# Scores of four more units from the split form in a recurrence with a feed-forward layer, on one core

## The chip, the cores and the metric

The kernel runs on one core of one Trainium2 chip. The metric is the device time of one execution in microseconds. Before the change it is 342.12 us, the median of three runs (340.52 to 343.04).

## The reference, cut to what matters

The first half is a gated linear recurrence, worked through in chunks of 32 tokens: 4 batches of 8 heads with 768 tokens, head width 32 and state width 16. The second half is a feed-forward layer with softplus on the 3072 rows that the first half gives.

```python
CB = np.einsum('bhin,bhjn->bhij', Cc, Bc)          # the scores
M = CB * L                                         # weighed with the decays, causal
y_intra = np.einsum('bhij,bhjd->bhid', M, xc)
y_inter = np.einsum('bhin,bhnd->bhid', Cc, state) * decay_to_i[:, :, :, None]
...
h = x @ w_in                                       # 256 -> 2048
g = np.maximum(h, 0.0) + np.log1p(np.exp(-np.abs(h)))
return (g @ w_out).astype(np.float32)              # 2048 -> 256
```

## The kernel before, in words

**Units.** The recurrence is cut into 24 units of 128 tokens of one batch, all 8 heads at once (unit i is batch i // 6, place i % 6). A unit's inputs are one load into a tile un: its tokens' x and B by token, C by row, and what the scores are made of. A unit goes through: rm, the causal decays, on POOL (`decays`, L345); the scores sp, two blocks of 128x512 for four heads each (`score`, L378); m, their product with rm, on DVE (`weigh`, L402); bp and cc, B and C scaled, on DVE (`scale_b`, L360, and `scale_c`, L376); zp and the new state (`update`, L416 and L428); tb, the state spread over two heads (`spread`, L436); the output yp, from the state (`read`, L450) and from m (`within`, L466); y, with the growth factors gg (L477), and its high and low parts xh and xl (L480, L485), which the layer reads.

**Two forms of scores.** Units 0 to 11 (`i < FIRST`) take each block as one plain float32 product: 64 rows of B against 512 columns of C that the host has laid out apart for each head (L386; units 0 to 3 from a tile of their own). Their load comes from the array fst, 576 KB a unit. Units 12 to 23 take the split form. Their load comes from the array un, 768 KB, with B and C stacked so that each number stands in several rows. `split_unit` makes from them, with one pass on ACT (L247) and one on DVE (L248) each, the tiles c_all and b_rows, which hold a number's high part in some rows and its low part in others. Two DMAs copy c_all into c_rows (L254, by the helper at L136), where each copy fills the rows of one of two heads and the rest stays zero. Then four products of 128 rows against 256 columns (L391) give the same two blocks. There is only one c_rows: it can be filled for a unit when the scores of the unit before have been taken. c_all and b_rows have two buffers each, un has three.

**The layer.** Six token blocks j of 512 tokens and 16 slices k of the 2048 hidden columns. For each (j, k) there are six products into hp (`first`, L563), with the weights' and the tokens' high and low parts wih, wil, xh, xl; then e, softplus, on ACT (L591), its high part gh on ACT (L597) and its low part gl on DVE (L603); then six products into the two sums acc (`second`, `block`, L642). The weights w_in and w_out arrive as 64-bit numbers; for each of 16 steps ACT and DVE turn them into high and low parts (`split_stages`): even steps make wih and wil, step 12 those of slices 12 and 13; odd steps make woh and wol. Tiles for e have three buffers, for gh and gl four.

**Order.** All loads, copies and stores go through one queue, issued by SP in the order of the list. Up to unit 7, and to the weights' last step, the order is written by hand (the table ORDER; its instructions appear at L127, the helper that records them, whatever function made them). From unit 8 on, and from the layer's step 20, the order is a plan: a loop over steps s (one (j, k) each) plans for unit 8 the scores at step 20, for units 9, 10 and 11 at 22, 25 and 28, for later ones every fourth step; the output part comes one step later for units 8 to 11 and two for the others; the load of unit i + 2 comes one step after unit i's scores (L767 to L773). Within that plan a scheduler places the instructions on each engine, so that an edit can move other work; instructions of the hand-written part and of the plan stand mixed on the engines around 76 to 92 us.

Of the kernel before, what the change touches and what calls it, by code (L numbers as in the profile page):

```python
# [26 lines left out]
NFT = DFF // P  # L27
TOK = NB * S
HEAD = 4
FIRST = 12  # L30
GU = 3
U_X = 0
U_B = U_X + DM
# [71 lines left out]
def recurrence_then_ffn(ctx: ExitStack, tc: tile.TileContext, fst, un, at, al, w_in, w_out, const, outT):  # L105
# [28 lines left out]
    def load(out, in_):  # L134

        tc.keep_in_program_order(nc.sync.dma_start(out, in_))  # L136
# [73 lines left out]
    def load_unit(i):  # L210
# [4 lines left out]
        un_s[i] = p3.tile([P, U_END], F32, tag="un", name=f"un{i}")  # L215
        if i < FIRST:
            load(un_s[i][:, :F_END], fst[i])
        else:
            load(un_s[i], un[i - FIRST])

# [17 lines left out]
    def split_unit(i):  # L238
        if i < FIRST:
            return  # L240
        t = un_s[i]
        b_rows = p2.tile([P, NQ, P], F32R, tag="b_rows", name=f"b_rows{i}")

        def split(out, j):
            raw = t[:, U_S + j * NQ * P : U_S + (j + 1) * NQ * P].rearrange("p (q t) -> p q t", q=NQ)
            g, be = (kb[:, C_GB + v : C_GB + v + 1] for v in (2 * j, 2 * j + 1))
            A.activation(out, raw, AF.Copy, scale=be)  # L247
            V.scalar_tensor_tensor(out, raw, g, out.bitcast(F32), op0=ALU.mult, op1=ALU.add)  # L248

        c_all = p2.tile([P, NQ, P], F32R, tag="c_all", name=f"c_all{i}")  # L250
        split(c_all, 1)
        for e in range(2):
            rows = slice(64 * e, 64 * e + 64)
            load(c_rows[rows, :, e].bitcast(F32), c_all[rows].bitcast(F32))  # L254
        split(b_rows, 0)
        st[i] = b_rows
# [121 lines left out]
    def score(i, g):  # L378
        sp = mid[i]["sp", g] = ps.tile([P, 512], F32, tag="ps", name=f"sp{i}_{g}")
        if i < FIRST:  # L380
            rows = slice(64 * g, 64 * g + 64)
# [452 lines left out]
```

## Time and profile before

| | |
|---|---|
| median of three runs | 342.12 us (340.52 to 343.04) |
| the profiled execution | 340.56 us, its span 338.8 us |
| PE busy | 328.7 us, 97% of the span |
| DVE, ACT, POOL busy | 202.8 (60%), 171.7 (51%), 39.3 (12%) us |
| chain that ended last | PE 86%, DVE 6%, DMA 5% |
| loads from fst, from un | 8 of 576 KB, 12 of 768 KB |
| granted TensorE clock | 1.00 |

How to read the rows: PE is the matrix engine's products, PEld its weight loads, DVE the vector engine, ACT the scalar engine, POOL GpSimd, SPq the queue of SyncE, which issues the DMAs. A row of a timeline has the start in us, the length in us, the engine, the line, the operation, what it writes <- what it reads, shapes, how many were merged, and in brackets how long the engine sat idle before it and what ended that. In these rows tiles have no numbers. A float32 product shows as two instructions. A product's length contains the pipeline's fill, so that lengths overlap; prices are taken from start to start. A window's row has its bounds and length, then the busy time and count of PE, PEld, DVE, ACT and POOL, the granted clock, the share of the 16 DMA engines' time and GB/s. A row of waits has who waited, for whom, the sum in us, how often, and the longest. A row of DMA issues has the number, the KB of each and the median us from issue to landing.

### The profile page before, as it was taken

The page shows a single profiled execution, that of the slowest core. Times are in us where ns is not written, and L with a number is a line of the kernel's source. Part 1 is how long each engine was busy: PE and PEld are TensorE (multiplying, and loading weights), DVE is VectorE, ACT ScalarE, POOL GpSimd, SP SyncE. Part 2 cuts the span into 40 slices and gives each one's busy share as a digit, 9 for nine tenths or more (in the row PEclk, how much of TensorE's full clock was granted, in tenths as well). Part 3 has the DMA queues.
Part 4 walks back from the last instruction along what each step waited for, and adds up shares of the span by engine and source line. Part 5 has one row for each costly group of instructions (what it writes and reads, how often), then busy time and mean ns, then how long its engine had stood idle before and what let it go on. Part 6 is the DMA issues. An engine that isn't in the chain of part 4 may idle for free.

```text
span 338.8 us, 5271 instructions
## 1 busy us (share of the span) xinstructions
PE 328.7 (97%) x2047; PEld 249.4 (74%) x2047; DVE 202.8 (60%) x394; ACT 171.7 (51%) x319; POOL 39.3 (12%) x32
## 2 busy tenths in 40 slices
PE   8789998999999999999999999999999999999995
PEld 4446657887666678778778778778778778888885
DVE  0899989996946444864765464777474342232242
ACT  4845666875715435445445455445445244444450
POOL 2434510000111010110112010111010000000000
PEclk9999999999999999999999999999999999999999
DMA  7964533573032205416434205443203100010001
GB/s 233 396 228 138 220 106 104 188 259 120 3 98 114 93 0 189 133 39 186 126 61 141 95 0 188 122 106 99 94 2 93 33 0 0 2 55 8 2 0 62
DMA packets 19376, 35.01 MB, mean 103 GB/s; under 512 B 1432, under 2 KB 10136, under 8 KB 19352
## 3 DMA queue, kind: packets, MB, share of 16 engines
q1 hardware_dynamic: 19352, 34.68, 31.5%
q8 instruction: 16, 0.26, 0.3%
q14 instruction: 8, 0.07, 0.1%
HBM read 28.28 MB, written 3.24 MB: 93 GB/s over the span
## 4 chain that ended last, share of the span: by engine, by line
PE 86%; DVE 6%; DMA 5%; SPq 1%; issue 1%; ACT 0%
PE hp L563 32%; PE acc L642 32%; PE hp L127 6%; PE acc L127 6%; PE yp L466 3%; DMA gg<-gd 3%; DMA head_in_l<-in_fst 2%; PE yp L450 2%; PE sp L391 2%; DVE m L127 1%; DVE w L127 1%; PE sp L386 1%; SPq L136 1%; PE zp L416 1%; PE end L127 1%
## 5 line engine op out<-in xcount | busy, mean ns | idle before, releaser
L603 DVE TENSOR_TENSOR gl<-e,gh 128x512 fp32r<-128x512 f32 x76 | 55.7, 734 | 61.3 <-ACT gh L597 61.1
L597 ACT CAST gh<-e 128x512 fp32r<-128x512 f32 x76 | 47.1, 620 | 61.1 <-PE acc L642 60.3
L591 ACT ACTIVATE e<-hp 128x512 f32<-128x512 f32 x76 | 45.1, 596 | 42.4 <-DVE gl L603 38.5
L563 PE MATMUL hp<-xh,wih 128*128 128x512 f32 x152 | 61.3, 405 | 0.0
L642 PE MATMUL acc<-gl,woh 128*128 128x512 f32 x155 | 60.6, 391 | 0.0
L642 PE MATMUL acc<-gh,wol 128*128 128x512 f32 x155 | 60.5, 391 | 0.0
L642 PE MATMUL acc<-gh,woh 128*128 128x512 f32 x155 | 59.6, 391 | 0.0
L563 PE MATMUL hp<-xl,wih 128*128 128x512 f32 x152 | 59.5, 392 | 0.0
L563 PE MATMUL hp<-xh,wil 128*128 128x512 f32 x152 | 59.3, 391 | 0.0
L345 POOL TENSOR_SCALAR_AFFINE_SELECT rm<-fc 128x1024 f32<-128x1024 f32 x16 | 23.8, 1487 | 187.7 <-DVE m L402 167.8
L563 PEld LDWEIGHTS hp<-xh,wih 128*128 128x128 f32 x152 | 28.5, 188 | 10.7 <-issue 3.1
L642 PEld LDWEIGHTS acc<-gh,woh 128*128 128x128 f32 x155 | 29.1, 188 | 6.8 <-issue 0.8
L642 PEld LDWEIGHTS acc<-gh,wol 128*128 128x128 f32 x155 | 29.1, 188 | 6.2
L642 PEld LDWEIGHTS acc<-gl,woh 128*128 128x128 f32 x155 | 29.1, 188 | 6.1 <-issue 0.2
L563 PEld LDWEIGHTS hp<-xh,wil 128*128 128x128 f32 x152 | 28.5, 188 | 6.3
L563 PEld LDWEIGHTS hp<-xl,wih 128*128 128x128 f32 x152 | 28.6, 188 | 5.1
L402 DVE TENSOR_TENSOR m<-sp,rm 128x512 f32<-128x512 f32 x32 | 20.9, 685 | 7.9 <-PE sp L391 6.3
L127 DVE SCALAR_TENSOR_TENSOR w<-wraw,w 128x512 int32<-128x512 int32 x32 | 23.1, 729 | 0.2
L127 PE MATMUL hp<-xh,wih 128*128 128x512 f32 (+1 forms) x48 | 17.7, 368 | 2.0 <-DVE m L127 1.4
L127 PE MATMUL hp<-xl,wih 128*128 128x512 f32 (+1 forms) x48 | 17.0, 354 | 0.0
L127 PE MATMUL hp<-xh,wil 128*128 128x512 f32 (+1 forms) x48 | 17.0, 354 | 0.0
L127 POOL TENSOR_SCALAR_AFFINE_SELECT rm<-fc 128x1024 f32<-128x1024 f32 x8 | 14.0, 1764 | 20.8 <-DVE m L127 15.0
(109 smaller groups left out, 409.6 us busy)
## 6 DMA issues: line engine op xcount, KB each, us to landing
un<-in_un SPq DMA_DIRECT2D x12, 768.0 KB, 4.4
un<-in_fst SPq DMA_DIRECT2D x8, 576.0 KB, 6.1
wraw<-in_w_in SPq DMA_DIRECT2D x8, 512.0 KB, 3.4
wraw<-in_w_out SPq DMA_DIRECT2D x8, 512.0 KB, 5.2
c_rows<-c_all SPq DMA_DIRECT2D x24, 128.0 KB, 2.4
out_t<-o SPq DMA_DIRECT2D x11, 256.0 KB
gg<-gd SPq DMA_DIRECT2D x14, 192.0 KB
head_in_l<-in_fst SPq DMA_DIRECT2D x4, 320.0 KB, 6.2
```

Source lines behind the costliest of these rows:

```text
L127: return lambda *a, **k: tc.keep_in_program_order(f(*a, **k))
L136: tc.keep_in_program_order(nc.sync.dma_start(out, in_))
L345: Pl.affine_select(out=rm.rearrange("p h c i -> p (h c) i"), in_=fc[:, u].rearrange("p h c -> p (h c)").unsqueeze(2).broadcast_to([P, NH * ...
L391: PE.matmul(sp[:, 2 * v * P : 2 * (v + 1) * P], b_rows[:, q], c_rows[:, q].rearrange("p e t -> p (e t)"), start=True, stop=True,)
L402: V.tensor_tensor(mid[i]["m"][:, 4 * g : 4 * g + 4].rearrange("p h t -> p (h t)"), mid[i].pop(("sp", g)), mid[i]["rm"][:, 4 * g : 4 * g + ...
L450: PE.matmul(yp[q // 2][out], tb[rows].rearrange("p e d -> p (e d)"), cc[rows].rearrange("p c i -> p (c i)"), start=True, stop=False,)
L466: PE.matmul(yp[g][32 * hh : 32 * hh + 32], un_s[i][:, U_X + h * D : U_X + (h + 1) * D], m[:, h, :], start=u == 0, stop=True,)
L563: PE.matmul(h[:, c0:c1], w[:, c, fs], x[:, c, c0:c1], start=i == 0, stop=i == 5)
L591: A.activation(e, h, AF.Softplus)
L597: A.copy(gh, e)
L603: V.tensor_tensor(gl, e, gh.bitcast(F32), op=ALU.subtract)
L642: PE.matmul(acc[:, c0:c1], wo[v, k // HK][:, k % HK, es], g[:, c0:c1], start=start and i == 0, stop=stop and i == 2,)
```

## The change

The number of the first unit in split form goes from 12 to 8.

```diff
-FIRST = 12
+FIRST = 8
```

All that depends on it follows: the host puts units 8 to 11 into the array un instead of fst; `load_unit` loads 768 KB for each of them instead of 576; `split_unit`, which returned at once for them, now makes c_all and b_rows and copies into c_rows; `score` takes the four products from c_rows and b_rows instead of two from un.

```python
def split_unit(i):
    if i < FIRST:
        return
...
def score(i, g):
    sp = mid[i]["sp", g] = ps.tile([P, 512], F32, tag="ps", name=f"sp{i}_{g}")
    if i < FIRST:
...
```

How this moves instructions is shown at three places. In the rows, un10 is unit 10's tile, gh1_7 the gh of j = 1, k = 7; the last number is the tile's own and means nothing.

SP, after the last weights. Before:

```order
L136 DMA un8_1062<-in_fst 128x1152
L136 DMA un9_1064<-in_fst 128x1152
L136 DMA gg9_1066<-gd_84 128x1x384 x2
L136 DMA un10_1138<-in_fst 128x1152
L136 DMA un11_1207<-in_fst 128x1152
L136 DMA un12_1309<-in_un 128x1536
```

And now:

```order
L136 DMA un8_1062<-in_un 128x1536
L136 DMA un9_1064<-in_un 128x1536
L136 DMA gg9_1066<-gd_84 128x1x384 x2
L136 DMA c_rows_86<-c_all8_1083 64x4x128 x2
L136 DMA un10_1148<-in_un 128x1536
L136 DMA c_rows_86<-c_all9_1164 64x4x128 x2
L136 DMA un11_1227<-in_un 128x1536
L136 DMA c_rows_86<-c_all10_1270 64x4x128 x2
L136 DMA un12_1339<-in_un 128x1536
```

Two copies into c_rows stand ahead of each load from un10 on.

ACT, where the hand-written part ends. Here e, gh and half belong to the layer, woh1 and wih to the weights (w15 and w12 are their steps 15 and 12). Before:

```order
L127 CAST gh1_6_988<-e1_6_892 128x512
L127 ACTIVATE e0_9_997<-hp0_9_910 128x512
L127 CAST woh1_855<-w15_952 128x512
L127 CAST gh1_7_1003<-e1_7_984 128x512
L127 ACTIVATE e0_11_1014<-hp0_11_934 128x512
L127 CAST wih_78<-w12_956 128x2x256
```

And now:

```order
L127 CAST gh1_6_988<-e1_6_892 128x512
L247 ACTIVATE c_all10_1270<-un10_1148,kb_77 128x512
L127 ACTIVATE e0_9_997<-hp0_9_910 128x512
L127 CAST woh1_855<-w15_952 128x512
L127 CAST gh1_7_1003<-e1_7_984 128x512
L127 ACTIVATE e0_11_1014<-hp0_11_934 128x512
L127 CAST wih_78<-w12_956 128x2x256
```

The pass for c_all10, which reads un10, stands ahead of five others. (On DVE, gl1_6 has gone from behind bp10 and cc10, which read un10, to ahead of them.)

PE, unit 8's state and output. Before, with zp8 on its own eight products into hp earlier:

```order
L416 MATMUL zp8_1110<-un8_1062,bp8_1091 32x64 x4
...
L450 MATMUL yp8_0_1117<-cc8_1093,tb8_1108 64x128 x2
L450 MATMUL yp8_1_1118<-cc8_1093,tb8_1108 64x128 x2
L466 MATMUL yp8_0_1117<-m8_1086,un8_1062 32x128 x4
L466 MATMUL yp8_1_1118<-m8_1086,un8_1062 32x128 x4
```

And now:

```order
L416 MATMUL zp8_1120<-un8_1062,bp8_1101 32x64 x4
L450 MATMUL yp8_0_1127<-cc8_1103,tb8_1118 64x128 x2
L466 MATMUL yp8_0_1127<-m8_1095,un8_1062 32x128 x4
L450 MATMUL yp8_1_1128<-cc8_1103,tb8_1118 64x128 x2
L466 MATMUL yp8_1_1128<-m8_1095,un8_1062 32x128 x4
```

The parts from the state (L450) and from m (L466) now alternate, directly behind zp8. Before, it was unit 10's that alternated; now unit 9's are cut by one product into hp.

## The prediction

> **What bounds the kernel now.** I read first the page's busy times and the chain that ended last, then busy time by stage, then the timelines of PE, ACT, DVE and the DMA issues around the first four planned units.
>
> ```profile
> PE 328.7 (97%) x2047; PEld 249.4 (74%) x2047; DVE 202.8 (60%) x394; ACT 171.7 (51%) x319; POOL 39.3 (12%) x32
> PE 86%; DVE 6%; DMA 5%; SPq 1%; issue 1%; ACT 0%
> ```
>
> ```profile
> 77.00:86.00 9.00, 9.00 (x47) 7.05 (x46) 6.65 (x15) 5.47 (x11) 0.00 (x0) 1.00 0.35 103
> 86.00:123.00 37.00, 37.00 (x247) 24.07 (x246) 22.46 (x47) 17.57 (x32) 5.13 (x4) 1.00 0.20 70
> 134.00:275.00 141.00, 141.00 (x905) 111.12 (x904) 85.39 (x162) 68.28 (x121) 15.44 (x10) 1.00 0.31 91
> ```
>
> In the windows the third number is PE's busy time: it equals the window's length in all three. Units 8 to 11 are scored in the second. So from 77 us on PE has no idle time to absorb anything: a microsecond taken from PE's work there comes off the end, and a microsecond that PE is made to wait is added to it. DVE (22.46 of 37) and ACT (17.57 of 37) have room as sums, but each works through its own list in order, so what counts is where a late input stands in the list.
>
> **What the change removes from PE.** The price of a score block is the start-to-start time across it, less that of two ordinary 128x512 products.
>
> ```profile
> 94.28 0.40 PE L563 MATMUL hp<-xh,wil 128*128 128x512 f32 x1
> 94.60 1.13 PE L386 MATMUL sp<-un 64*128 64x512 f32 x4
> 95.66 0.50 PE L642 MATMUL acc<-gh,woh 128*128 128x512 f32 x1
> 96.00 0.40 PE L642 MATMUL acc<-gl,woh 128*128 128x512 f32 x1
> ```
>
> ```profile
> 133.61 0.39 PE L642 MATMUL acc<-gh,wol 128*128 128x512 f32 x1
> 133.84 0.64 PE L391 MATMUL sp<-c_rows,b_rows 128*128 128x256 f32 x4
> 134.31 0.40 PE L563 MATMUL hp<-xh,wih 128*128 128x512 f32 x1
> 134.54 0.40 PE L563 MATMUL hp<-xl,wih 128*128 128x512 f32 x1
> ```
>
> Ordinary products start 0.227 us apart (133.61 to 133.84 is such a step). Plain scores of unit 9: 96.00 - 94.28 - 2 x 0.227 = 1.27 us. Split scores of unit 12: 134.54 - 133.61 - 2 x 0.227 = 0.48 us. Four units save 4 x 0.79 = **3.2 us** of PE.
>
> [...]
>
> **What the reorder costs PE.** The scheduler also places the output products anew. Unit 8's, in one piece before, are now interleaved (state part, own part, state part, own part); unit 10's, interleaved before, no longer are.
>
> ```profile
> 98.39 0.45 PE L450 MATMUL yp<-cc,tb 32*64 32x128 f32 x8
> 99.34 0.50 PE L563 MATMUL hp<-xh,wih 128*128 128x512 f32 x1
> ```
>
> ```profile
> 109.53 0.43 PE L450 MATMUL yp<-cc,tb 32*64 32x128 f32 x4
> 110.23 0.43 PE L450 MATMUL yp<-cc,tb 32*64 32x128 f32 x4
> 111.16 0.50 PE L563 MATMUL hp<-xh,wih 128*128 128x512 f32 x1
> ```
>
> In one piece 99.34 - 98.39 = 0.95 us, interleaved 111.16 - 109.53 = 1.63 us. Units 8 and 10 exchange that 0.68, and unit 9's block is newly cut by one hidden-layer product. Bounds: 0 (they cancel) to +0.7 (one more interleaved block). I take **+0.4**: the exchange cancels, and unit 9's single cut is priced at a little over half of the 0.68 that two cuts cost.
>
> **What it adds, and what hides it.** Per unit two passes on ACT, two on DVE, two copies into c_rows, and 192 KB more in the load.
>
> ```profile
> 103.73 0.72 ACT L247 ACTIVATE c_all<-un,kb 128x512 fp32r<-128x512 f32 x1 [0.19 <-DMA un<-in_un]
> 104.36 0.71 ACT L247 ACTIVATE b_rows<-un,kb 128x512 fp32r<-128x512 f32 x1
> 104.49 0.75 DVE L248 SCALAR_TENSOR_TENSOR c_all<-un,kb,c_all 128x512 fp32r<-128x512 f32 x1 [0.46 <-ACT c_all L247]
> ```
>
> As work this is 4 x 1.43 = 5.7 us of ACT and some 6 us of DVE, beside 19 us and 14 us idle on them in 86 to 123: nothing, with that cover. If the cover were gone (every pass in PE's way) it would be 12 us; I see no place for that, except one.
>
> **The new wait.** ACT's list now has c_all10 ahead of e0_9, woh1 (step 15), gh1_7, e0_11 and wih (step 12). c_all10 cannot start before un10 has landed, and the five behind it wait with it. Two of them are PE's: acc takes gh1_7, and hp0_12, the product right after, takes wih of step 12.
>
> ```profile
> 79.50 0.62 ACT L127 CAST gh<-e 128x512 fp32r<-128x512 f32 x1 [1.22 <-PE acc L127]
> 80.03 0.59 ACT L127 ACTIVATE e<-hp 128x512 f32<-128x512 f32 x1
> 81.39 0.59 ACT L127 ACTIVATE e<-hp 128x512 f32<-128x512 f32 x1
> 81.88 0.61 ACT L127 CAST woh<-w 128x512 fp32r<-128x512 f32 x1
> 82.39 0.62 ACT L127 CAST gh<-e 128x512 fp32r<-128x512 f32 x1
> 84.83 0.60 ACT L127 ACTIVATE e<-hp 128x512 f32<-128x512 f32 x1 [1.82 <-DVE gl L127]
> 85.44 0.62 ACT L127 CAST wih<-w 128x512 fp32r<-128x512 f32 x1
> ```
>
> ```profile
> 83.71 0.29 DVE L360 TENSOR_TENSOR bp<-un,ft 128x128 f32<-128x128 f32 x1 [2.26 <-DMA un<-in_fst]
> ```
>
> ```profile
> 86.35 0.39 PE L563 MATMUL hp<-xh,wih 128*128 128x512 f32 x1
> ```
>
> ```profile
> ACT c_all L247 <- DMA un<-in_un: 11.9, 11, 2.4
> ```
>
> Before, un10 (landed by 83.71) held up bp10 on DVE, gl1_6 behind it, and so e0_11; wih ended at 85.44 + 0.62 = 86.06 and PE took it at 86.35: a margin of 0.29 us. That such a pass idles ACT until its load is in, the last row shows for the later units (11 waits). Now, from un10's landing to the end of wih: c_all10 0.63 (103.73 to 104.36), e0_9 0.49 (81.39 to 81.88), woh1 0.51, gh1_7 0.53 (79.50 to 80.03), e0_11 0.61, wih 0.62, together **3.4 us**. The copies and the DVE passes for e0_11 and wih are ready earlier: gl1_6 now stands ahead of bp10, and the last DVE pass for step 12, behind bp10 and another short one, ends about 1.2 us after the landing (an estimate: 0.2 us for each short one, about 0.7 for the pass).
>
> **When un10 lands.** It waits for unit 7's buffer as before, but stands on SP behind the two copies into c_rows.
>
> ```profile
> 77.94 0.33 SPq L136 DMA_DIRECT2D un<-in_fst  x1
> ```
>
> ```profile
> 72.00:77.00 5.00, 5.00 (x23) 4.13 (x22) 4.51 (x9) 3.71 (x7) 0.00 (x0) 1.00 0.89 345
> ```
>
> ```profile
> 135.80:137.30 1.50, 1.50 (x9) 1.23 (x8) 1.50 (x3) 1.50 (x4) 0.30 (x1) 1.00 0.86 172
> 104.00:108.00 4.00, 4.00 (x17) 2.63 (x17) 3.24 (x6) 2.18 (x4) 0.14 (x1) 1.00 0.22 76
> ```
>
> ```profile
> un<-in_un SPq DMA_DIRECT2D x12, 768.0 KB, 4.4
> un<-in_fst SPq DMA_DIRECT2D x8, 576.0 KB, 6.1
> c_rows<-c_all SPq DMA_DIRECT2D x24, 128.0 KB, 2.4
> ```
>
> Issued at 77.94, un10 took 5.8 us, because the growth factors (two gg copies) were still in the queue: the last window, after un12 has landed, shows such a pair keep 0.22 of the DMA engines busy for 4 us at 76 GB/s. My reading is that un10's share on those few engines comes after gg. Then what is put ahead adds up there: un8 and un9 192 KB more each at 345 GB/s, 1.1 us; the c_rows pair 1.5 us (the 135.80 window, 172 GB/s, holds nearly that pair alone); un10's own 192 KB, 0.6 us. Landing at 83.7 + 1.1 + 1.5 + 0.6 = 86.9. Bounds: 83.7 (all of it passes on engines that are free) and 90.2 (the two copies cost their landing time of 2.4 us each instead of 1.5 together). I take 86.9, because every term has a row of the same kind of transfer.
>
> hp0_12 then starts at 86.9 + 3.4 = 90.3 instead of 86.35: **+4.0 us** (0.8 to 7.3 by the bounds). What is late next: sp8 needs c_rows8, which is ahead of un10 in the queue and so in by then. gl1_7, the step-12 wil and m8 come off DVE some 3 to 6 us after the landing, counting its list at 0.6 to 0.75 us a pass, and PE, counting its list at 0.227 us a product, asks for them 5 to 8 us after it. From there c_rows9 waits for sp8, un11 behind it for unit 8's products, and m9's second half, on DVE behind c_all11, for un11: with the 4.4 us of the un row and one pass each on ACT and DVE it is done about 1 us before PE asks for it. These are estimates from the rows shown, and I take nothing for them.
>
> **Sum.** 340.56 (profiled execution, span 338.8 and 1.76 around it) + 4.0 - 3.2 + 0.4 = 341.8, +1.2 us. Against the median of the runs, 342.12, that is **343.3 us**. A measurement tells about 1% (3.4 us) from no change, so this is no change.
>
> **The rivals.**
>
> *The load is not late (340.1 us).* un10 lands at 83.7 as before. For it: at a share of 0.22, some 12 of the 16 DMA engines are free in the gg tail. Against: un10's own 5.8 us in that tail. Price: 83.7 + 3.4 - 86.35 = 0.8 us of wait, net -2.0; with no wait at all -2.8, or 339.3.
> [...]
>
> *The copies block the queue (346.6 us, slower).* One mechanism: the c_rows pair, in small pieces, goes at 2.4 us a copy on the engines that gg holds, and un10 lands at 90.2. hp0_12 waits 7.3 us, net +4.5. It decides (over 1%) once un10 lands after 89.1. For it: the landing time of 2.4 us. Against: the pair took 1.5 us together at 135.80, with no gg beside it.
>
> *The wait ends elsewhere, no net change (342.1 us).* The saved 3.2 us come back as small waits at m9, m10 and yp, whose inputs now hang on c_rows and on loads behind it in SP's list. For it: the slack of about 1 us at m9. Against: no single one is long.
>
> **How the numbers follow.** Forecast 0.55, load not late 0.25, copies block 0.12, scattered waits 0.08. Faster by over 1% needs more than the whole PE saving without any wait: only the far edge of the second case, 0.06. Slower by over 1%: the third case and the edge of the forecast, 0.14. Same 0.80. The range goes from the second case's 340.1, a little below for the spread of the runs (339.8), to 345.5, short of the third case.
>
> **What would show it.** Right: sp of units 8 to 11 as L391 rows with 0.48 us each; c_all10 on ACT idle before it for 3 us or more, released by the load of un10; then one PE gap of 3 to 5 us just ahead of acc with gh1_7 and hp0_12, between 85 and 92 us, and none as long after it; PE full again from there, the end shifted by the gap less 2.8. Wrong: no PE gap there (second case); a gap over 6 us (third); a bp10 that starts before 85 us; or gaps at sp9, yp9 or yp10.

## The result

The changed kernel takes **344.35 us** (median of 20 executions, 341.54 to 349.05), the kernel before, measured beside it, 341.01 us (339.86 to 343.04): a ratio of **1.0081, interval 1.0057 to 1.0104**. It is a little slower, 3.3 us by the medians. The forecast was 343.3 us, 1.2 us more than the 342.12 that three executions of before had given; on the median of the 20 it would be 342.2.

The profiled execution of the changed kernel (span 347.3 us) was disturbed in its first 22 us (half clock from 11.7 to 15.1 and from 18.5 to 21.9 us), ahead of anything that the change touches; so a second profiled execution of the same kernel, the first of the experiments, is read beside it; the ratios leave disturbed executions out, and so differ a little from the quotients of the medians. The second's busy times and its chain:

```profile
PE 331.3 (96%) x2047; PEld 253.5 (74%) x2047; DVE 212.0 (62%) x402; ACT 175.9 (51%) x327; POOL 40.2 (12%) x32
PE 86%; DMA 5%; DVE 4%; ACT 2%; issue 1%; POOL 1%; SPq 0%; ACTq 0%; DVEq 0%; POOLq 0%
```

PE has as many products as before, eight passes more stand on DVE and eight on ACT, and PE still carries the chain. PE's busy time has risen, 328.7 to 331.3 us, although its scores became cheaper, because products at half clock take longer (0.43 us from start to start instead of 0.227, shown below). Not all of that is the change's: this execution ran at half clock also from 15.7 to 19.2 and from 49.8 to 53.3 us, ahead of anything that the change touches. The changed kernel by stage, in the first execution (bounds and length, then busy time of PE, PEld, DVE, ACT and POOL, the granted clock, DMA share, GB/s):

```profile
82.90:93.60 10.70, 8.74 (x45) 6.84 (x44) 8.67 (x19) 5.88 (x12) 0.00 (x0) 1.00 0.47 132
93.60:100.50 6.90, 6.08 (x16) 4.63 (x17) 6.21 (x10) 4.94 (x11) 1.67 (x1) 0.51 0.20 39
100.50:142.30 41.80, 41.80 (x278) 31.40 (x277) 25.52 (x49) 19.57 (x36) 4.87 (x3) 1.00 0.39 117
```

In the first window PE is idle for 2 us, in the second for 0.8 more, and there **the granted clock is 0.51**. From 100.5 us on PE is full at full clock. The same stages in the second execution, up to where PE is full at full clock again:

```profile
80.60:94.20 13.60, 10.52 (x54) 8.17 (x54) 11.43 (x25) 7.96 (x16) 0.00 (x0) 1.00 0.36 104
94.20:97.60 3.40, 3.40 (x10) 2.63 (x9) 3.40 (x4) 3.27 (x7) 1.67 (x1) 0.50 0.43 84
```

The gap is where it was forecast. ACT's timeline in the second execution (start, length, operation, idle time before it and what ended that):

```profile
84.27 0.61 ACT L127 CAST gh<-e 128x512 fp32r<-128x512 f32 x1
89.63 0.72 ACT L247 ACTIVATE c_all<-un,kb 128x512 fp32r<-128x512 f32 x1 [4.75 <-DMA un<-in_un]
90.26 0.58 ACT L127 ACTIVATE e<-hp 128x512 f32<-128x512 f32 x1
90.73 0.61 ACT L127 CAST woh<-w 128x512 fp32r<-128x512 f32 x1
91.24 0.62 ACT L127 CAST gh<-e 128x512 fp32r<-128x512 f32 x1
91.76 0.60 ACT L127 ACTIVATE e<-hp 128x512 f32<-128x512 f32 x1
92.25 0.61 ACT L127 CAST wih<-w 128x512 fp32r<-128x512 f32 x1
```

c_all10 waits 4.75 us for un10, and the five passes behind it follow without a break. PE's timeline beside it:

```profile
88.95 0.39 PE L127 MATMUL acc<-gh,wol 128*128 128x512 f32 x1
91.91 0.50 PE L127 MATMUL acc<-gh,woh 128*128 128x512 f32 x1 [2.58 <-ACT gh L127]
92.92 0.50 PE L563 MATMUL hp<-xh,wih 128*128 128x512 f32 x1 [0.50 <-ACT wih L127]
...
94.19 0.58 PE L563 MATMUL hp<-xl,wih 128*128 128x512 f32 x1
94.57 0.63 PE L127 MATMUL acc<-gl,woh 128*128 128x512 f32 x1
...
97.56 0.44 PE L563 MATMUL hp<-xl,wih 128*128 128x512 f32 x1
```

PE waits 2.58 us for gh1_7 and 0.50 for wih of step 12 (2.56 and 0.21 us in the first execution). What the forecast lacks stands below that: from 94.19 to 97.56 the products start 0.43 us apart, not 0.227. Eight of them take 3.37 us where 8 x 0.227 = 1.82: **1.55 us lost to the clock**. In the first execution ten products and a score block take 5.27 us from 95.21 to 100.48, where 10 x 0.227 + 0.48 = 2.75: 2.5 us lost.

To compare executions whose starts differ, I use one **stretch** of PE's timeline: from the start of zp7 to the first score of unit 12. Before, it is 77.56 to 133.84, 56.28 us. From its end to PE's last product every kernel here takes 201.32 us (one, named below, 200.0). What differs ahead of zp7 is scatter of the first 55 us and has nothing to do with the change (from acc with its gap of 0.85 us there, at 51.94 us before and 57.33 now, zp7 is 25.6 us away in both), but it is in the medians.

| kernel | median us | ratio to before, interval | stretch us | PE gaps after 80 us | clock there |
|---|---|---|---|---|---|
| before | 341.01 | | 56.28 | none | 1.00 |
| changed | 344.35 | 1.0081 [1.0057, 1.0104] | 59.40 | 2.56, 0.21 | half for 6.83 us |
| changed, again | 345.18 | 1.0092 [1.0053, 1.0131] | 58.59 | 2.58, 0.50 | half for 3.41 us |
| twelve dummy products | 342.21 | 1.0008 [0.9972, 1.0044] | 56.57 | 0.51 | 1.00 |
| six dummy products | 343.60 | 1.0070 [1.0030, 1.0111] | 57.23 | 1.11, 0.51 | 1.00 |
| growth factors behind un10 | 339.75 | 0.9947 [0.9911, 0.9983] | 54.29 | 0.50 | 1.00 |
| unit 10's passes kept late | 342.74 | 1.0022 [0.9995, 1.0048] | 58.08 | 0.81, 0.36, 1.64 | 1.00 |
| un10 first | **339.14** | **0.9934 [0.9911, 0.9958]** | 54.23 | 0.43, 0.26 | 1.00 |
| un10 ahead of the copies only | 344.84 | 1.0101 [1.0067, 1.0134] | 59.24 | 2.06, 0.46, 0.21 | half for 6.83 us |
| before, with 768 KB loads | 342.22 | 1.0011 [0.9977, 1.0044] | 56.26 | none | 1.00 |
| FIRST = 11 | 341.91 | 1.0000 [0.9974, 1.0025] | 56.51 | 0.74 | 1.00 |
| FIRST = 10 | 340.30 | 1.0000 [0.9972, 1.0028] | 56.07 | 0.40, 0.50, 0.50 | 1.00 |

Each ratio is to the kernel before on the same chip in the same set of runs, whose medians there were 341.01 for the changed kernel, 342.06 for the first four experiments, 342.03 for the next four and 340.58 for the last two (six dummy products, FIRST = 10).

### The profile page after: what moved, and what is told of

It is laid out like the page before. It is cut to its first block, busy times and chain, and to the rows that moved or that the text cites. A ratio compares the mean times of both kernels' runs of the same rounds, so it can differ in the third digit from the quotient of the medians.

```text
span 347.3 us, 5310 instructions
## 1 busy us (share of the span) xinstructions
PE 332.4 (96%) x2047; PEld 253.7 (73%) x2047; DVE 211.2 (61%) x402; ACT 175.5 (51%) x327; POOL 40.2 (12%) x32
## 4 chain that ended last, share of the span: by engine, by line
PE 83%; DMA 7%; DVE 4%; ACT 2%; SPq 1%; issue 1%; ACTq 0%; DVEq 0%
PE hp L563 31%; PE acc L642 31%; PE hp L127 6%; PE acc L127 4%; DMA gg<-gd 3%; PE yp L466 3%; PE sp L391 2%; DMA head_in_l<-in_fst 2%; DMA un<-in_un 2%; PE yp L450 2%; PE sp L127 2%; DVE m L127 1%; SPq L136 1%; PE zp L416 1%; DVE w L127 1%
## 5 line engine op out<-in xcount | busy, mean ns | idle before, releaser
L563 PE MATMUL hp<-xl,wih 128*128 128x512 f32 x152 | 60.2, 396 | 0.0
L345 POOL TENSOR_SCALAR_AFFINE_SELECT rm<-fc 128x1024 f32<-128x1024 f32 x16 | 24.7, 1542 | 190.9 <-DVE m L402 178.7
L247 ACT ACTIVATE c_all<-un,kb 128x512 fp32r<-128x512 f32 x16 | 11.6, 724 | 21.2 <-DMA un<-in_un 19.0
L248 DVE SCALAR_TENSOR_TENSOR b_rows<-un,kb,b_rows 128x512 fp32r<-128x512 f32 x16 | 19.0, 1189 | 0.3
```

The lines of the kernel that those rows point to most:

```text
L345: Pl.affine_select(out=rm.rearrange("p h c i -> p (h c) i"), in_=fc[:, u].rearrange("p h c -> p (h c)").unsqueeze(2).broadcast_to([P, NH * ...
L563: PE.matmul(h[:, c0:c1], w[:, c, fs], x[:, c, c0:c1], start=i == 0, stop=i == 5)
```

## The experiments

**1. The changed kernel again**, no edit, to have a second trace.

> The changed kernel once more, for a profile of another execution. The theory: PE idles for about 2.7 us ahead of acc with gh1_7 because c_all10 holds ACT until un10 has landed; right behind that gap the granted clock is 0.5 for one or two windows of 3.4 us, which costs PE another 1.7 to 3.4 us; together with the 2.8 us that the split scores save this gives 343 to 345 us, some 0.8% over the kernel before. The rival: the slow clock belonged to that one execution, and the loss is in waits elsewhere; then this profile shows a granted clock of 1.00 behind the gap and still 344 us.

Measured: ratio 1.0092, the stretch 58.59 us. The gap is there again (2.58 and 0.50 us), the half clock lasts 3.41 us instead of 6.83. The gap belongs to the kernel; how much the clock adds differs from one execution to the next.

**2. Twelve dummy products** on PE just ahead of the product that takes gh1_7. Nothing reads them; they only keep PE busy where it waited.

```diff
-... Z1.6 P0.8 P0.11 P0.10 Z1.7 P0.10 P0.8 K1
+... Z1.6 P0.8 P0.11 P0.10 pad12 Z1.7 P0.10 P0.8 K1
```

> Twelve products without use, 2.7 us of work at 0.22 us each, stand on PE just ahead of acc with gh1_7, where PE would idle. ACT's wait for un10 is as it was. The theory (the idle time is what lowers the clock): the granted clock stays 1.00 in 86 to 106 us, hp0_12 starts no later than before, and only the slow clock's part is saved: 341 to 342 us, about 3 us less than the changed kernel. The rival (the clock falls for another reason, or the loss is all wait): 344 us or more.

PE's timeline:

```profile
87.36 2.76 PE L127 MATMUL pad<-some 128*32 128x512 bf16 x12
90.21 0.49 PE L127 MATMUL acc<-gh,woh 128*128 128x512 f32 x1
91.22 0.50 PE L574 MATMUL hp<-xh,wih 128*128 128x512 f32 x1 [0.51 <-ACT wih L127]
```

```profile
91.20:98.00 6.80, 6.78 (x57) 5.18 (x58) 6.53 (x11) 5.58 (x11) 1.61 (x1) 1.00 0.21 42
```

The first product of step 12 is as late as without them (12.50 us behind zp7's start, 12.30 without), so the wait is not shortened at all. But the clock stays at 1.00 from 91.2 to 98.0 us, where the second execution of the changed kernel has 0.50 behind its gap, and the kernel is 3.0 us faster than the changed one in the same set of runs (342.21 against 345.18). The other executions agree: mean clocks of 0.993 to 1.00 in its ten, 0.984 to 0.995 in the five of the changed kernel. The stretch is 2.0 us shorter than in the second execution. Not all of that is the clock: the scheduler placed the output products anew, and from the start of each yp row to the next row they take 4.50 us over the stretch here, 5.13 there. The other 1.4 us, with the first product of step 12 0.2 us later here, fit the 1.55 that the clock cost in that trace. PE's work that does nothing pays here: with it in the gap the clock read 1.00, without it 0.50. So the clock is a cost of its own, behind the gap and not in it.

**3. The growth factors behind un10.** The two gg copies are issued after un10 instead of ahead of it; c_rows8 stays ahead.

```diff
     for i in range(EARLY, EARLY + 2):
-        prefetch(i)
+        load_unit(i)
+    plan(U_STEP[0] + 1, load_growth, EARLY + 1)
```

> The two gg copies for units 9 to 11 are issued behind un10 instead of ahead of it; ACT's order is as in the changed kernel. The theory (un10 is late since it stands behind gg and the c_rows pair on a few DMA engines): un10 lands 2 to 3 us earlier, about 4.5 us after its issue instead of 7.3; PE's gap shrinks to below 1 us, the clock stays 1.00, and the time is 339 to 340 us, 1 to 2 us below the kernel before. The rival (un10 is late for its own size and late issue, gg does not matter): landing 7 us after issue as before, 344 us.

SP's and ACT's timelines:

```profile
82.34 0.61 SPq L136 DMA_DIRECT2D un<-in_un  x1
83.00 1.16 SPq L136 DMA_DIRECT2D gg<-gd  x2
```

```profile
87.18 0.73 ACT L247 ACTIVATE c_all<-un,kb 128x512 fp32r<-128x512 f32 x1 [2.10 <-issue]
```

un10 is there at most 4.84 us after its issue (82.34 to 87.18), where the changed kernel has 82.19 to 89.63, 7.44 us, with the same copies into c_rows ahead. Of the gap 0.50 us is left, the clock is 1.00 (products start 0.23 us apart behind it), the ratio 0.9947. That the gg copies delay un10, which the prediction only read into a window, is shown by this; by how much, within the scatter that the run with FIRST = 11 shows.

**4. Unit 10's passes kept late**: c_all10, b_rows10, bp10 and cc10 may not be placed ahead of the hand-written part. The load stays as it is.

```diff
+            in_order[0] = i == EARLY + 2
             A.activation(out, raw, AF.Copy, scale=be)
+            in_order[0] = False
...
+        in_order[0] = i == EARLY + 2
         scale_b(i)
         scale_c(i)
+        in_order[0] = False
```

> Unit 10's two passes on ACT and its bp and cc on DVE are kept behind the hand-written part, so that nothing of the weights or of block 1 waits for un10; the loads are as in the changed kernel, un10 as late as there. The theory (the order on ACT is what turns the late load into a PE wait): no PE gap ahead of acc with gh1_7, clock 1.00, all of the saving kept: 338 to 339 us, 2.5 to 3 us below the kernel before. The rival (the late load reaches PE in any order, through sp10 or c_rows10 further on): a new PE gap near sp10 or yp10 and 341 us or more.

The gap at gh1_7 is gone, but PE waits later:

```profile
125.68 0.71 PE L393 MATMUL sp<-c_rows,b_rows 128*128 128x256 f32 x4 [1.64 <-DMA c_rows<-c_all]
```

The copies into c_rows come late now, and the scores of unit 11 wait 1.64 us for them. The two other gaps, 0.81 and 0.36 us, are ahead of it, near 114 and 116 us. The stretch is 58.08, after which this kernel alone takes 200.0 us: over both it is 0.5 us longer than before. The theory's 338 to 339 us is missed. The wait has moved, as the rival had it, though to the scores of unit 11 and not to sp10 or yp10; the gap of 1.64 us leaves the clock alone: behind it, from 126.70 to 127.84, products start 0.23 us apart.

**5. un10 first**: un10 right behind un9, then the copies of c_rows8, then gg9.

```diff
-        if i + 2 < NB * NU:
+        if EARLY < i and i + 2 < NB * NU:
             plan(s + 1, prefetch, i + 2)
-    for i in range(EARLY, EARLY + 2):
-        prefetch(i)
+    for i in range(EARLY, EARLY + 3):
+        load_unit(i)
+    plan(U_STEP[0] + 1, load_growth, EARLY + 1)
```

> The changed kernel with un10 issued right behind un9, ahead of the copies into c_rows, and the gg copies behind both. The theory: un10 lands about 4.5 us after its issue and before ACT comes to c_all10, so that PE has no gap of more than 0.3 us ahead of hp0_12 and the whole saving of the split scores stays, less the dearer order of the output products: 2.5 to 3 us below the kernel before, 338 to 339 us. The rival (some 0.8 us of waiting stays as behind gg_late, since c_all10 and the three passes after it are simply too many for ACT there): 2 us below, the same as with gg late.

```profile
77.81 0.33 SPq L136 DMA_DIRECT2D un<-in_un  x1
78.24 1.37 SPq L136 DMA_DIRECT2D c_rows<-c_all  x2
79.66 1.20 SPq L136 DMA_DIRECT2D gg<-gd  x2
```

```profile
83.12 0.29 DVE L360 TENSOR_TENSOR bp<-un,ft 128x128 f32<-128x128 f32 x1 [0.42 <-DMA un<-in_un]
```

```profile
84.10 0.72 ACT L247 ACTIVATE c_all<-un,kb 128x512 fp32r<-128x512 f32 x1 [2.19 <-DMA c_rows<-c_all]
```

un10 lands 5.3 us after its issue. c_all10 starts only 1 us later, because now something else is last: it takes the buffer of c_all8, which the copies must have read first. PE still waits 0.43 and 0.26 us. The stretch is 54.23, 2.05 us shorter than before, the rival's 2 and not the theory's 2.5 to 3, and no half clock follows (1.00 from 87.4 to 131.6 us). This kernel **beats both**: 339.14 us, ratio 0.9934, interval 0.9911 to 0.9958.

**6. un10 ahead of the copies only**: gg9 stays ahead of un10, c_rows8 goes behind it.

```diff
         prefetch(i)
+    load_unit(EARLY + 2)
```

(and the condition `EARLY < i` as in the run before).

> The changed kernel with un10 issued ahead of the copies into c_rows for unit 8, but behind the two gg copies. It prices the c_rows pair in the queue. The theory as predicted (the pair costs un10 1.5 us on the engines that gg holds): the PE gap ahead of acc with gh1_7 shrinks from 2.6 to about 1.1 us and the clock stays at 1.00: 341 to 342 us. The rival (the pair passes almost free, the gg copies alone make un10 late): a gap of 1.9 us or more, with or without a slow window, 342 to 345 us.

```profile
80.63 15.09 SPq L136 DMA_DIRECT2D c_rows<-c_all  x4
```

```profile
88.29 0.29 DVE L360 TENSOR_TENSOR bp<-un,ft 128x128 f32<-128x128 f32 x1 [2.13 <-DMA un<-in_un]
...
88.70 0.69 DVE L127 TENSOR_TENSOR gl<-e,gh 128x512 fp32r<-128x512 f32 x1
```

```profile
89.05 0.72 ACT L247 ACTIVATE c_all<-un,kb 128x512 fp32r<-128x512 f32 x1 [4.89 <-DMA c_rows<-c_all]
```

```profile
89.44 0.50 PE L127 MATMUL acc<-gl,woh 128*128 128x512 f32 x1 [2.06 <-DVE gl L127]
91.33 0.80 PE L127 MATMUL acc<-gh,woh 128*128 128x512 f32 x1 [0.46 <-ACT gh L127]
```

un10 lands 8.5 us behind zp7's start instead of 8.9, so this place in the queue is worth 0.4 us, against 3.2 us in the run before (5.7 us behind zp7's start), where un10 went ahead of gg9 too. (Four traces with the changed kernel's queue have 8.86 to 9.13.) Issued 1.2 us earlier, it only took longer, 8.1 us to bp10 instead of 7.4. And c_all10 gains nothing: it starts at 89.05, 9.2 us behind zp7's start where the changed kernel has 9.0, because the copies, issued at 80.63, are now the last that it waits for. The scheduler moved something besides: gl1_6 stands behind bp10 on DVE, so PE waits there first. A gap of 2.06 us, and half clock for 6.83 us: 344.84, as the rival had it.

**7. The bytes alone**: the kernel before, with loads of 768 KB for units 8 to 11 (the added columns are zeros that nothing reads).

```diff
-        if i < FIRST:
-            load(un_s[i][:, :F_END], fst[i])
+        if i < EARLY:
+            load(un_s[i][:, :F_END], fst[i, :, :F_END])
+        elif i < FIRST:
+            load(un_s[i], fst[i])
```

> The kernel before (units 8 to 11 with plain scores), with their loads made 768 KB by columns of zeros that nothing reads: the added bytes alone. The theory: un10 lands 1.5 to 1.8 us later than before and its late passes on DVE delay wih of step 12 and hp0_12 by 0.5 to 1.5 us; no slow clock: 0.5 to 1.5 us above the kernel before. The rival (the bytes pass on free engines): no change. If the bytes were the main cost: 3 us or more above.

```profile
81.50 0.33 SPq L136 DMA_DIRECT2D un<-in_fst  x1
```

```profile
88.90 0.29 DVE L362 TENSOR_TENSOR bp<-un,ft 128x128 f32<-128x128 f32 x1 [1.98 <-DMA un<-in_fst]
```

un10 takes 7.4 us from issue to bp10, where it took 5.77 before: 1.6 us more. It cost PE nothing (the rival's time, but not its reason), because in this build the last pass for step 12 and gl1_6 stand ahead of bp10 and ACT has no pass that reads un10 there.

**8. FIRST = 11**: unit 11 alone changes form.

```diff
-FIRST = 12
+FIRST = 11
```

> Only unit 11 in split form (first split unit 11). Its c_all stands far behind the hand-written part and un10's load is as before, so neither the ACT wait nor the slow clock can come. The theory: a quarter of the saving, 0.7 to 0.8 us, 0.2% below the kernel before, which is at the edge of what can be told. The rival (the split form itself costs PE more than its 0.79 us saves, by waits on c_rows): no gain or a loss.

Ratio 1.0000, the stretch 56.51, 0.2 us longer than before, in place of the 0.8 us that one unit's scores save. PE has one gap, 0.74 us ahead of acc with gl1_6, which the scheduler left behind bp10. un10, of 576 KB as before, took 6.8 us here from issue (80.13) to bp10 (86.92), against 5.77 before. So this time scatters by about 1 us with the same loads, and of the 1.6 us of the run above between 0.6 and 1.6 are the bytes'. Nothing waits for c_rows, so the rival's reason is not there; that the ratio shows no gain comes from this gap.

**9. Six dummy products** instead of twelve, to leave a shorter gap.

```diff
-... P0.8 P0.11 P0.10 Z1.7 P0.10 P0.8 K1
+... P0.8 P0.11 P0.10 pad6 Z1.7 P0.10 P0.8 K1
```

> The change with six dummy products (128x32 against 128x512, bf16, nothing reads them) ahead of the product that takes gh1_7, where the run before had twelve; nothing of the kernel's own work is left out. Twelve took 2.76 us and closed the 2.58 us gap. Six should take 1.38 us and leave a gap of about 1.2 us there. Theory (the clock halves only behind a gap of over 2 us): no window of half clock behind it, the stretch from zp7 to the first score of unit 12 at 56.6 us as with twelve, median 342.2, ratio 1.000. Rival (any gap of over 1 us there halves the clock): a window of half clock, the stretch at 58.3 to 59.4, median 344 to 345, ratio 1.007.

```profile
88.09 1.47 PE L127 MATMUL pad<-some 128*32 128x512 bf16 x6
90.67 0.49 PE L127 MATMUL acc<-gh,woh 128*128 128x512 f32 x1 [1.11 <-ACT gh L127]
91.68 0.51 PE L574 MATMUL hp<-xh,wih 128*128 128x512 f32 x1 [0.51 <-ACT wih L127]
```

The gap is 1.11 us as meant, and no half clock follows it in the trace (1.00 from 85 to 137 us); the stretch is 57.23, nearer to the theory's 56.6 than to the rival's 58.3. (The scheduler interleaved more of the output products in this build, four pieces for unit 8 where the run with twelve has two: over the stretch they take 5.33 us against 4.50, which is more than the whole difference of 0.66.) But the median, 343.6 and 1.007, is the rival's figure. 1.9 us of it lie ahead of zp7 in the profiled execution (79.45 against 77.56); whether the other executions have the half clock behind the gap now and then, one trace cannot tell. The mean clocks of the seven, 0.984 to 1.00 where twelve products gave 0.993 to 1.00, speak for it, but do not say where in the execution the clock fell. This run is for the theory by its trace and undecided by its median.

**10. FIRST = 10**: units 10 and 11 alone change form.

> FIRST = 10: units 10 and 11 alone change form; nothing is left out. PE saves 2 x 0.79 = 1.6 us. ACT has the passes for c_all10 and b_rows10 ahead of the five that wait; un8 and un9 are loads of 576 KB and no copy into c_rows stands ahead of un10, whose own bytes are 192 KB more. Theory (the price is un10's landing and ACT's chain behind it): un10 lands 0.6 us later than before, the chain takes 3.4 + 0.6 us, wih of step 12 ends at 84.3 + 4.0 = 88.3 on the clock of before, where PE takes it at 86.35: a gap of about 2.0 us in one or two pieces, net +0.4: median 342.4, ratio 1.001; if that gap halves the clock for a window, +2.1: 344.1, ratio 1.006. Rival (ACT's list is not what holds PE, the scheduler's other moves are): no gap ahead of gh1_7 and step 12's first product, net -1.6, 340.4, ratio 0.995.

```profile
86.03 0.72 ACT L247 ACTIVATE c_all<-un,kb 128x512 fp32r<-128x512 f32 x1 [3.10 <-DMA un<-in_un]
...
89.27 0.61 ACT L127 CAST wih<-w 128x512 fp32r<-128x512 f32 x1
```

```profile
86.98 0.50 PE L127 MATMUL acc<-gl,woh 128*128 128x512 f32 x1 [0.40 <-DVE gl L127]
88.93 0.50 PE L127 MATMUL acc<-gh,woh 128*128 128x512 f32 x1 [0.50 <-ACT gh L127]
89.93 0.50 PE L563 MATMUL hp<-xh,wih 128*128 128x512 f32 x1 [0.50 <-ACT wih L127]
```

wih ends at 89.88, 10.88 us behind zp7's start at 79.00: on the clock of before 88.4, where 88.3 was expected. The first product of step 12 comes 2.1 us later than before, and the ratio is 1.0000 against the theory's 1.001; 0.995, without the wait, lies outside the interval. The size of the gap was a miss: 1.4 us of idle time in three pieces, not 2.0. The rest of the 2.1 us is overlap that each gap breaks: from 88.93 to 89.93 two products start 1.00 us apart, of which 0.50 is idle and 0.227 the usual step. No half clock follows (1.00 from 91 to 135 us).

## Why the prediction was nearly right, point by point

**The saving on PE, -3.2 us: right.** A split score block of unit 10 in the changed kernel:

```profile
115.13 0.39 PE L642 MATMUL acc<-gh,woh 128*128 128x512 f32 x1
115.36 0.64 PE L391 MATMUL sp<-c_rows,b_rows 128*128 128x256 f32 x4
115.83 0.40 PE L642 MATMUL acc<-gl,woh 128*128 128x512 f32 x1
116.06 0.40 PE L563 MATMUL hp<-xh,wih 128*128 128x512 f32 x1
```

116.06 - 115.13 - 2 x 0.227 = 0.48 us, the forecast's figure to the hundredth.

**The wait: in its place and of its kind.** By the second execution, counted from zp7's start:

| step | forecast | measured |
|---|---|---|
| un10's landing later by | 3.2 us | 8.9 - 6.15 = 2.8 us (89.55, bp10's start, and 80.62; 83.71 and 77.56) |
| landing to the first product of step 12 | 3.4 us | 89.55 to 92.92, 3.4 us |
| that product later by | 4.0 us | 12.30 - 8.79 = 3.5 us |
| PE idle there | 3 to 5 us | 2.58 + 0.50 = 3.1 us |

The landing's terms are confirmed as a sum and not one by one. un10 is issued 1.2 us later (1.57 us behind zp7's start, 0.38 before), since SP issues the c_rows pair first, and takes 7.4 us to bp10 instead of 5.8. The bytes account for 0.6 to 1.6 us of the latter, by the runs with 768 KB loads and with FIRST = 11. Putting the pair behind un10 gave back 0.4 us, so 1.5 us was too much for its place in the queue. The 3.5 us are more than the 3.1 of idle time, because around each gap the overlap of two products is lost: from 91.91 to 92.92 two of them start 1.01 us apart, of which 0.50 is idle and 0.227 the usual step.

**The reorder, +0.4 us: fits.** It is what remains of the stretch: 58.59 - 56.28 + 3.2 - 3.5 - 1.55, some 0.4 in the second execution, 59.40 - 56.28 + 3.2 - 3.5 - 2.5 = 0.3 in the first. The rows show it too: from the start of each yp row to the next row, the output products take 4.84 us over the stretch before and 5.13 in the second execution, 0.3 more. The exchange does not quite cancel (units 8 and 10 together 2.58 us before, 2.74 now), and unit 9's cut costs 0.13.

**What was wrong: "PE full again from there, the end shifted by the gap less 2.8".** PE is full again, but at a clock of 0.50 for 3.41 us in one execution and 6.83 us in the other. That term, **+1.6 to +2.5 us**, is missing from the sum. With it the stretch is 2.3 and 3.1 us longer, about what the median shows (3.3). The executions without a trace agree: two of the 20 have a mean clock of 1.00, with spans of 339.8 and 340.4 us; the kernel before, at clocks of 0.997 or more, has a median span of 338.7 us (35 executions in three sets of runs). That is 1.1 to 1.7 us, near the predicted 1.2 where the clock stays whole, though two executions are few. So the half clock is frequent behind this gap and not certain.

That 343.3 us lies only 1.1 from the measured 344.35 is partly luck. The forecast stood on a median of three, 342.12, which is 1.1 us above the median of the 20, and its wait of 4.0 us was 0.5 too long; both hid part of the missing term.

I had seen the granted clock at 1.00 in every window of before and took it as a constant. From 77 us on PE had no gap there, and the run with twelve dummy products, at 1.00 behind this place where the changed kernel has 0.50, shows that the clock there hangs on that.

The places that the prediction gave as signs of a wrong one, sp9, yp9 and yp10, made no gap, nor did m9. The first rival, a load that is not late, is refuted by the landing 2.8 us later; the second, copies that block the queue, because the landing is at 86.5 on the clock of before, where it needed 89.1; the third, scattered waits, is not in these traces, but waits of its kind came when unit 10's passes were held back.

## What to carry to other kernels

Price a new gap on a full PE at more than its length where the trace shows the clock fall behind it: here the products behind gaps of 2.06 to 2.58 us ran at a clock of 0.50 for 3.41 or 6.83 us, which cost the changed kernel 1.55 and 2.5 us, and twelve useless products in the gap won that part back. When a change puts a pass that reads a load ahead of others on an engine (here the five passes behind c_all10 waited 4.75 us with it), look at where that load stands in its queue: here issuing un10 ahead of copies that are needed later turned 0.8% slower into 0.7% faster. And read a stretch of the trace beside the median, since the scatter of other parts is as large as the effect.

## What the runs showed of the hardware

**The granted clock fell at four gaps of 2.06 to 2.58 us.** Half clock began within 2.3 us of the end of those of 2.06 us (un10 ahead of the copies only), 2.10 (the first execution of the changed kernel, at 11.24 us) and 2.58 (the second), and inside that of 2.56 (the first). At 1.7 us it went both ways. The second execution of the changed kernel has one near 49 us, in the part that no edit touches:

```profile
49.06 0.45 PE L127 MATMUL yp<-cc,tb 32*64 32x128 f32 x8 [1.74 <-DVE tb L127]
49.44 0.50 PE L127 MATMUL hp<-xh,wih 128*128 128x512 f32 x1
...
50.13 0.63 PE L127 MATMUL hp<-xh,wil 128*128 128x512 f32 x1
50.56 0.63 PE L127 MATMUL hp<-xh,wih 128*128 128x512 f32 x1
```

The first execution has 1.67 us at the same place and stays at 1.00:

```profile
49.00:58.00 9.00, 6.48 (x46) 3.91 (x46) 6.78 (x15) 4.59 (x9) 1.61 (x1) 1.00 0.33 105
```

Behind the gaps of 1.64, 1.41 and 1.11 us (unit 10's passes kept late; the first execution, at 28.59 us; six dummy products) no half clock follows. But it can come without such a gap: the first execution also has 0.50 from 18.5 to 21.9 us, where in the 7 us ahead PE has no gap over 0.31 us; why, stays open. Such losses are not the change's alone: of the 65 executions of the kernel before in the sets of the experiments, 30 have a mean clock under 0.997, and 3.41 us at half clock lower the mean by 0.005 (0.5 x 3.41 of some 340 us). What decides between 1.67 and 1.74 us is not shown.

**Two small copies held a large load up.** The gg copies, 192 KB each, ahead of un10 cost it some 2.6 us (7.44 us from issue against at most 4.84 without them). The two runs with un10 ahead of the c_rows copies say the same: it lands 8.5 us behind zp7's start with gg ahead of it and 5.7 without. Meanwhile half of the DMA engines' time went unused (in the second execution a share of 0.51 and 156 GB/s from 84.3 to 89.5 us, most of which is ACT's wait). Small copies fare no better: the c_rows pair, 128 KB each with a median of 2.4 us to landing, took 8.4 us behind gg and un10 (80.63 to 89.05).
